# The first of twelve steps put in another order, and the sign of w_out's words set by VectorE

## The chip, the cores and the metric

The kernel runs on one core of one Trainium2 chip. The metric is the device time of one execution, in microseconds. Three unprofiled executions before the change took 602.38, 602.40 and 603.73 us; their median, 602.4 us, is the time before.

## What is computed

A recurrent attention layer (RWKV6) feeds a feed-forward block with an unusual gate:

```python
for t in range(S):                                   # S = 768, batch 4, 8 heads, head size 48
    kt, vt, rt, wt = k[:, :, t], v[:, :, t], r[:, :, t], w[:, :, t]
    cur = einsum('bhd,bhe->bhde', u * kt, vt)
    y[:, :, t] = einsum('bhd,bhde->bhe', rt, state + cur)
    state = wt[..., None] * state + einsum('bhd,bhe->bhde', kt, vt)
x = y.transpose(0, 2, 1, 3).reshape(3072, 384)
h = x @ w_in                                         # 384 -> 2048
g = h * erf(softplus(h))
out = g @ w_out                                      # 2048 -> 384
```

All inputs of the attention are fp32. `w_in` and `w_out` reach the kernel as doubles and are made fp32 on the chip.

## The kernel before

The work is cut into 12 steps; step s holds 128 tokens of two batch entries (16 heads). The recurrence is not run token by token. Inside a step the tokens are combined in levels 1 to 6 (spans of 2, 4, ... 64 tokens). For a level, TensorE makes 64 small products of r and k (`level_products`), VectorE then multiplies r and k by running products of w (`scale`), and VectorE or ScalarE takes the wanted part of the products into the tile `own` (`take_level`). The next level's products need the scaled r and k, and write into the other of two PSUM tiles, `pp0` and `pp1`, once its reader is done. The running products of w, the "totals", are made by GpSimd: one multiplication of neighbours per level, 512, 256, ... 16 columns wide, in `prepare`. After level 6 comes the end of the attention step: `from_own` (own times v), the transposes of K with the copies into `kT`, `state_part` (K times v, the new state), and `through_state` (the old state times r). The result goes into `xT`, and the feed-forward block of step s-1 (`hidden`, L947) and of step s-3 (`project`, L979, later `project_fast`, L1055) runs between the levels of step s. Steps 0 to 3 take all six levels this way; later steps do the near tokens on VectorE and GpSimd from other tiles (`rows`).

Every engine executes its own list in the order in which the program issues it: the kernel switches the scheduler off for all five engines, so the order in the source is the order on each engine, and an instruction that waits holds up all behind it on its engine. That goes for SyncE's list of loads too. Some loads are held back on purpose by a tiny GpSimd copy into the first word of the destination tile, which reads a tile that is written late (`load(i, behind)`, `load_v(s, behind)`, `wait_for`).

The weights come in 16 pairs of 128-row blocks, 0 to 7 of `w_in` and 8 to 15 of `w_out`, as pairs of 32-bit words. Each pair goes through stages that carry one letter: `l` loads the words (three buffers, `words`), `b` scales the high words on ScalarE into PSUM (L245), `r` scales the low words on ScalarE into `rest` (L254), `h` shifts the scaled high words left by three on VectorE (L262), `o` adds `rest` on GpSimd (L270), and `j` is `h` and `o`. Pairs 0 and 1 use the PSUM tiles `m` in two halves, the others the PSUM tile `y`, one after another. `b` is a Prelu whose slope for negative numbers puts the sign where the shift keeps it[...]. The table `CONVERT` says which stages run in steps 1, 2 and 3 at which level, each entry with two strings: ahead of `take_level`, and in `place`, behind it.

Step 0 (`attend_first`, L702) has no other work beside it but the first two weight pairs. `keep_busy` (L806) issues two matmuls of zeros, 384 and 192 columns wide, into a `pp` tile that nobody reads, one such pair in each of levels 2 to 5. The second half of step 0's state, `pending` (L789), is run in step 1.

Of the kernel before, what the change touches and what calls it, by code (L numbers as in the profile page):

```python
# [17 lines left out]
P = 128  # L18
# [43 lines left out]
def kernel(  # L62
# [105 lines left out]
    def load_second(behind):  # L168

        t = ins.tile([P, 2, JP, C], FP32, name="in")  # L170
        vt = ins.tile([P, NH, D], FP32, name="v")
        ws[1] = ins.tile([P, JP, C], FP32, name="w")
        loaded[1] = t, vt
        nc.scalar.copy(t[:, 0, 0, 0:1], behind)
        load_halves(t, rkw[1])
        nc.sync.dma_start(out=ws[1][:], in_=rkw[1][:, 2])

    def load_v(s, behind=None):

# [36 lines left out]
    def convert(weights):  # L216

        held = {}  # L220
        plain = weights[0][1].dtype == FP32

        def load(i, behind=None):
            if i >= len(weights):
                return
            dst, src = weights[i]
            if plain:
                nc.sync.dma_start(out=dst, in_=src)
                return
            words = wide.tile([P, 2, DM, 2], I32, name="words", bufs=3)  # L230
            if behind is not None:
                nc.gpsimd.tensor_copy(out=words[:, 0, 0, 0:1].bitcast(FP32), in_=behind)
            load_halves(words[:].rearrange("p i n two -> p i (n two)"), src.bitcast(I32))
            held[i] = {"words": words}

        def scale_high(i, part=slice(0, 2)):


            if i not in held:
                return  # L240
            if i < 2:
                base = ps_m.tile([P, NP * C], FP32, name="m")[:, :DM]
            else:
                base = y[:].rearrange("p e j q t -> p e (j q t)")[:, :, :DM]
            nc.scalar.activation(  # L245
                base, held[i]["words"][:, part, :, 1].bitcast(FP32), AF.Prelu,
                scale=2.0**-112, alpha=-(2.0**32),
            )
            held[i].setdefault("bases", []).append((base.bitcast(I32), part))

        def scale_low(i):
            if i in held:
                rest = wide.tile([P, 2, DM], I32, name="rest", bufs=2)
                nc.scalar.mul(  # L254
                    out=rest[:], in_=held[i]["words"][:, :, :, 0].bitcast(U32), mul=2.0**-29
                )
                held[i]["rest"] = rest

        def shift(i):
            if i in held:  # L260
                base, part = held[i]["bases"].pop(0)
                nc.vector.tensor_scalar(  # L262
                    out=weights[i][0].bitcast(I32)[:, part], in0=base, scalar1=3, scalar2=None,
                    op0=ALU.logical_shift_left,
                )

        def add(i):
            if i in held:
                into = weights[i][0].bitcast(I32)
                nc.gpsimd.tensor_tensor(  # L270
                    out=into, in0=into, in1=held.pop(i)["rest"][:], op=ALU.add
                )

        def join(i):
            shift(i)
            add(i)

        stages = {"l": load, "b": scale_high, "r": scale_low, "h": shift, "o": add, "j": join}
        done = {"l": 4, "b": 2, "r": 2, "j": 2}

        def send(what):
            for stage in what:
                stages[stage](done[stage])
                done[stage] += 1

        return stages, send
# [10 lines left out]
    def scale(s, level, batch=None, only=None):  # L297
# [23 lines left out]
            halves, halves, view(tots[level - 1], 0, [[1, n], [2, nb], [0, half]])  # L321
        )

    def prepare(s):


        in_t = loaded[s][0]
        if s < DIRECT:
            rk1 = att.tile([P, 2, JP, C], FP32, name="rk1", bufs=1)
            parts = 1 if s else NJ  # L330
            def multiply_u(i, x):
                n = slice(i * JP // parts, (i + 1) * JP // parts)
# [21 lines left out]
            if s < 2:  # L354
                for i in range(parts):
                    for x in range(2):
                        multiply_u(i, x)
                yield
            else:
                yield  # L360
                yield
                multiply_u(0, 0)

        tots, tot = [], ws[s][:].rearrange("p n t -> p (n t)")
        tot_sb = att.tile([P, JP * (C - NC)], FP32, name="tot_sb")
# [1 line left out]
        for level in range(1, LOG + 1):  # L367
# [4 lines left out]
            nc.gpsimd.tensor_mul(new, pair[:, :, 0], pair[:, :, 1])  # L372
            tot = new
            used += nb
            if level == (2 if s > 1 else 1) and s < DIRECT:
                yield
        if s < DIRECT:
            ready[s] = rk1, tots, tot
            yield
            if s >= 2:  # L380
                yield
                multiply_u(0, 1)
            return

        own = att.tile([P, NH, HC], FP32, name="own")
# [316 lines left out]
    def attend_first(xT):  # L702


        c, in_t, vt, made, S, S_next, ends = parts_of(0)
        K = in_t[:, 1]
        RK = in_t[:, 0:2]
        following = prepare(1)
        own = att.tile([P, NH, HC], FP32, name="own")
        halves = [range(j * NP, (j + 1) * NP) for j in range(NJ)]  # L710

        def wait_for(of):

            nc.gpsimd.tensor_copy(out=block_sb[:, 0:1], in_=of)

        pp = products([P, NE, JP, HC])
        for half in halves:
            level_products(pp, made[:], 1, half)
            stay_warm(2)
        nc.scalar.copy(first[:], mask_sb[:, 0, :])  # L720
        for j in range(NJ):
            scale(0, 1, batch=j)
        load_second(in_t[:, 0, JP - 1, 1:2])
        nc.vector.tensor_mul(
            own[:], pp[:].rearrange("p e n t -> p (e n) t"),
            first[:, None, :].to_broadcast([P, NH, HC]),
        )
        for level in range(2, LOG):
            pp = turns.pop("pp", None) or products([P, NE, JP, HC])
            level_products(pp, RK, level)  # L730
# [4 lines left out]
            if level == 2:  # L735
                stages["b"](0, 0)
                stages["b"](0, 1)
                stages["r"](0)
                next(following)
            elif level == 3:  # L740
                stages["l"](1, own[:, 0, 4:5])
                stages["h"](0)
            elif level == 4:
                load_v(0, own[:, 0, 8:9])
                stages["h"](0)
                stages["b"](1, 0)
                stages["b"](1, 1)
                stages["r"](1)
                wait_for(in_t[:, 0, JP - 1, 8:9])
                next(following)  # L750
        pp = turns.pop("pp")
        level_products(pp, RK, LOG)
        for only in (1, 0):
            scale(0, LOG, only=only)
        take_level(own, pp, LOG)
        stages["l"](2, own[:, 0, HC // 2 : HC // 2 + 1])
        stages["l"](3)

        kT = att.tile([P, NH, D], FP32, name="kT", bufs=1)
        kT_by_e = kT[:].rearrange("p (e n) d -> p e n d", e=NE)  # L760
        turned = []
        for half in halves:
            turned.append(products([P, NP, P]))
            for i, n in enumerate(half):
                nc.tensor.transpose(turned[-1][:, i, :], K[:, n, :], ident[:])
        from_own(0, own, 1)
        stages["h"](1)
        for half, ps, copy in zip(halves, turned, (nc.scalar.copy, nc.vector.tensor_copy)):
            copy(
                kT_by_e[:, :, half.start : half.stop],  # L770
                ps[:].rearrange("p n (e d) -> p e n d", e=NE)[..., :D],
            )
        fence()
        ps = [[products([P, NE, JP, HC], 1 - e)[:, e] for e in range(NE)]]
        state_part(0, kT, ps, (0,))
        from_own(0, own, 0)
        nc.scalar.copy(middle[rows(1)], ps[0][1][rows(1), :, :D])
        nc.vector.tensor_copy(middle[rows(0)], ps[0][0][rows(0), :, :D])
        stages["h"](1)
        wait_for(in_t[:, 0, JP - 1, HC - 1 : HC])  # L780
        stages["o"](0)
        nc.gpsimd.tensor_mul(faded[1][:], middle[:], ends[:, :, 1:2].to_broadcast([P, JP, D]))
        stages["o"](1)
        load_v(1, middle[:, 0, 0:1])
        for _ in following:
            pass
        through_state(0, xT)

        def pending():  # L789
# [13 lines left out]
                start=True, stop=True,  # L803
            )

    def keep_busy(pp):  # L806

        zeros = states[1][0][:].rearrange("p n d -> p (n d)")
        for n in (DM, DM // 2):
            nc.tensor.matmul(  # L810
                pp[:].rearrange("p e n t -> p (e n t)")[:, :n], lhsT=ident[:],
                rhs=zeros[:, :n], start=True, stop=True, skip_group_check=True,
# [2 lines left out]
    def attend(s, xT, early, place, behind):  # L815
# [11 lines left out]
        for level in range(near_log(s) + 1 if s == DIRECT else 1, LOG + 1):  # L827
# [9 lines left out]
            if level == LOG and s == DIRECT:  # L837
                spread_blocks(s + 1, pp)
            scale(s, level)
            early(level - 1)  # L840
            got = pp[:].rearrange("p e n t -> p (e n) t")
            if level == 1:
# [2 lines left out]
                )  # L845
            else:
                take_level(own, pp, level)
            if s == 1 and level == LOG - 2:
                turns.pop("pending")()
                load_v(2)  # L850
            if level > 1 and (s, level) != (DIRECT, LOG - 1):
                next(following, None)
            place(level - 1)
# [288 lines left out]
    def run_late(s, tokens, following=None):  # L1142
# [26 lines left out]

    CONVERT = (  # L1170
        (),
        (("j", "brl"),) * 5 + (("j", ""), ("", ""), ("", ""), ("", "brl")),
        (("j", "brl"),) * 5 + (("j", "l"), ("", ""), ("", ""), ("", "br")),
        (("j", "br"), ("j", "")),
    )

    STAGES = {
# [17 lines left out]
    with tc.manual_schedule(  # L1195
# [12 lines left out]
            ]  # L1208
        )
        stages["l"](0, loaded[0][0][:, 1, JP - 1, C - 1 : C])  # L1210
        for _ in prepare(0):
            pass
        for s in range(n_steps):
            xTs[s] = xs.tile([P, KT, UNIT], FP32, name="xT")
            places = iter(range(8))
# [149 lines left out]
```

## Time and profile before

| what | value |
|---|---|
| median of three executions | 602.4 us |
| the profiled execution | 606.16 us |
| its span, first to last instruction | 604.4 us |
| TensorE (matmul) busy | 587.1 us, 97% |
| VectorE busy | 431.3 us, 71% |
| ScalarE busy | 363.7 us, 60% |
| GpSimd busy | 272.2 us, 45% |
| granted TensorE clock, mean | 0.991 |
| step 0's first matmul of `hidden` (L947) starts | 34.12 us |

Durations and gaps come from the profiled execution, which is 3.8 us above the median. A row of the timeline has the start, the duration, the engine, the line, the operation, what is written and read, and, in brackets, how long the engine sat idle before it and what ended that. In tables by window the columns are the busy time of each engine with the number of its instructions, the granted TensorE clock (1.00 is full), and the share and rate of the DMA engines.

### The profile page before, as it was taken

The numbers are of one execution on the slowest core, as the hardware profiler recorded it, in microseconds if no ns is written. First come the engines' busy times: TensorE is split into PE (matmuls) and PEld (weight loads), VectorE is DVE, ScalarE is ACT, GpSimd is POOL, SyncE is SP. The second block draws the span as 40 slices with busy tenths as digits, with TensorE's granted clock in tenths as the row PEclk, the third lists the DMA queues.
The fourth block names the chain that finished last, engine by engine and source line by source line (L and its number), as shares of the span: only waits on it lengthen the run. The fifth ranks groups of instructions, "written<-read, shape, count | busy, mean of one in ns | idle before, by whom it ended". The sixth has DMA issues, their size and how long they took to land.

```text
span 604.4 us, 16605 instructions
## 1 busy us (share of the span) xinstructions
PE 587.1 (97%) x7262; PEld 503.2 (83%) x7262; DVE 431.3 (71%) x510; ACT 363.7 (60%) x475; POOL 272.2 (45%) x303
## 2 busy tenths in 40 slices
PE   8898989999999999999999999999999999999997
PEld 6676768668757867899899899899898898898997
DVE  6756377599998599899799799799799624124140
ACT  3546777735436288684864865864765764656710
POOL 4357138250549729929729629639539100000000
PEclk9889999999999999999999999999999999999999
DMA  6684193504034323524334334324331300000000
GB/s 232 202 301 149 42 347 121 214 17 144 17 134 159 71 104 110 128 101 169 72 104 168 72 104 168 71 104 133 72 106 53 72 8 27 2 21 13 2 26 28
DMA packets 53937, 63.24 MB, mean 105 GB/s; under 512 B 35144, under 2 KB 40424, under 8 KB 52840
## 3 DMA queue, kind: packets, MB, share of 16 engines
q1 hardware_dynamic: 53480, 61.98, 31.9%
q8 instruction: 57, 0.93, 0.6%
q10 hardware_dynamic: 384, 0.20, 0.1%
q14 instruction: 16, 0.13, 0.1%
HBM read 52.39 MB, written 8.69 MB: 101 GB/s over the span
## 4 chain that ended last, share of the span: by engine, by line
PE 73%; DVE 11%; ACT 3%; issue 2%; DMA 1%; SPq 1%; ACTq 0%; POOL 0%; DVEq 0%; POOLq 0%
PE m L947 33%; PE m L1055 28%; PE m L979 4%; DVE in L320 3%; PE pp L509 2%; PE y L543 2%; DMA words<-in_moe_w_out 1%; PE y L569 1%; DVE sums L424 1%; PE pp L615 1%; DVE h L936 1%; DVE words L438 1%; DVE rk L434 1%; DVE mixed L1003 1%; DVE own L521 1%
## 5 line engine op out<-in xcount | busy, mean ns | idle before, releaser
L947 PE MATMUL m<-xT,w_in_sb 128*128 128x256 f32 x1152 | 258.7, 383 | 3.7 <-ACT h L956 2.7
L947 PEld LDWEIGHTS m<-xT,w_in_sb 128*128 128x128 f32 x1152 | 217.2, 191 | 35.3 <-ACT h L956 2.9
L956 ACT COPY h<-m 128x512 f32<-128x512 f32 x96 | 55.8, 581 | 85.2 <-PE m L947 85.1
L320 DVE TENSOR_TENSOR in<-in,tot_sb 128x1024 f32<-128x1024 f32 (+1 forms) x59 | 82.5, 1399 | 21.1 <-PE pp L509 13.5
L434 POOL TENSOR_TENSOR rk<-words 128x528 f32<-128x528 f32 (+3 forms) x28 | 41.5, 1481 | 91.5 <-DVE sums L424 81.1
L438 POOL TENSOR_TENSOR words<-words,rest 128x528 f32<-128x528 f32 (+10 forms) x77 | 79.0, 1026 | 6.0
L979 PE MATMUL m<-w_out_sb,h 128*128 128x384 f32 x192 | 64.3, 491 | 1.0 <-DVE h L936 1.0
L979 PEld LDWEIGHTS m<-w_out_sb,h 128*128 128x128 f32 x192 | 35.7, 190 | 24.6 <-issue 1.1
L1055 PE MATMUL m<-mixed,h 128*128 128x192 f32 x288 | 51.1, 331 | 0.0
L1055 PE MATMUL m<-w_out_sb,h 128*128 128x192 f32 x288 | 50.3, 329 | 0.0
L903 ACT ACT_TABLE_LOAD x36 | 46.2, 1283 | 2.6 <-DMA xT<-y 2.0
L1055 PEld LDWEIGHTS m<-w_out_sb,h 128*128 128x128 f32 x288 | 46.9, 190 | 0.5
L1055 PEld LDWEIGHTS m<-mixed,h 128*128 128x128 f32 x288 | 46.6, 190 | 0.9
L907 ACT ACT_TABLE_LOAD x36 | 46.2, 1283 | 1.6 <-DVE room L1038 1.1
L509 PEld LDWEIGHTS pp<-in 48*64 48x64 f32 (+1 forms) x2368 | 33.7, 126 | 15.1 <-issue 7.3
L372 POOL TENSOR_TENSOR tot_sb<-tot_sb 128x256 f32<-128x256 f32 (+4 forms) x60 | 42.5, 708 | 4.5
L1055 PE MATMUL m<-w_out_sb,room 128*128 128x192 f32 x256 | 44.2, 326 | 0.0
L509 PE MATMUL pp<-in 48*64 48x64 f32 (+1 forms) x2368 | 38.2, 212 | 4.3 <-issue 1.5
L1055 PEld LDWEIGHTS m<-w_out_sb,room 128*128 128x128 f32 x256 | 42.0, 190 | 0.0
L912 DVE TENSOR_TENSOR h<-h,y 128x1024 f32<-128x1024 f32 x17 | 20.7, 1215 | 28.3 <-ACT y L907 28.2
L903 ACT ACTIVATE room<-h 128x1024 f32<-128x1024 f32 x36 | 38.1, 1057 | 0.4
L434 POOL TENSOR_TENSOR words<-words 128x336 f32<-128x336 f32 (+6 forms) x49 | 35.3, 719 | 3.8
(139 smaller groups left out, 800.7 us busy)
## 6 DMA issues: line engine op xcount, KB each, us to landing
in<-in_rkw SPq DMA_DIRECT2D x8, 1024.0 KB, 5.1
words<-in_moe_w_in SPq DMA_DIRECT2D x16, 384.0 KB, 5.4
words<-in_moe_w_out SPq DMA_DIRECT2D x16, 384.0 KB, 6.1
words<-in_rk_rows SPq DMA_DIRECT2D x8, 768.0 KB, 5.7
w<-in_rkw SPq DMA_DIRECT2D x11, 512.0 KB, 5.7
v<-in_v SPq DMA_DIRECT2D x12, 384.0 KB, 6.1
out<-o SPq DMA_DIRECT2D x24, 192.0 KB, 2.6
in<-in_rkw SPq DMA_DIRECT2D x7, 512.0 KB, 5.4
```

Of the source, the lines that this page charges most:

```text
L320: nc.vector.tensor_mul(halves, halves, view(tots[level - 1], 0, [[1, n], [2, nb], [0, half]]))
L372: nc.gpsimd.tensor_mul(new, pair[:, :, 0], pair[:, :, 1])
L434: engine.tensor_mul(terms[n], r[:, :, n:], k[:, :, : near - n])
L438: engine.tensor_mul(k[:, :, :m], k[:, :, :m], w[:, :, n : n + m])
L509: nc.tensor.matmul(pp[s0 : s0 + m, e, n, :m], lhsT=rk[rows(e), 1, n, s0 : s0 + m], rhs=rk[rows(e), 0, n, t0 : t0 + m], start=True, stop=True,)
L903: nc.scalar.activation(sp_room, chunks[0], AF.Softplus)
L907: nc.scalar.activation(at, sp_room, AF.Erf)
L912: nc.vector.tensor_mul(h, h, at)
L947: nc.tensor.matmul(ps[:, ff, :], lhsT=w_in_sb[:, g * FG + f + ff, kk * P : (kk + 1) * P], rhs=xT[:, kk, :], start=kk == 0, stop=kk == KT - 1,)
L956: nc.scalar.copy(h[:, f : f + FT, :], ps[:])
L979: nc.tensor.matmul(ps[j][:], lhsT=gs[g][:, f, j * C : (j + 1) * C], rhs=w_out_sb[:, g * FG + f, :], start=g + f == 0, stop=g == NG - 1 and ...
L1055: nc.tensor.matmul(to, lhsT=a[:, f], rhs=b[:, f], start=start and f == 0, stop=f == FG - 1, skip_group_check=True,)
```

## The change

- **GpSimd's totals of step 0** are no longer made in one go. `plan_totals` lays them out, and `attend_first` issues level 1 in two halves (one as soon as half of w is there, one behind the scaling of level 1), and levels 2 to 6 behind the scalings of levels 2, 3 and 4, each behind a `wait_for` copy. The totals of step 1 move behind the middle state.
- **Loads**: v of step 0 and w of step 1 are issued in level 2, behind the words of pair 1, whose load moves from level 3 to level 2. v of step 1 is issued ahead of pair 1's addition.
- **Pair 1's scalings** (`b`, `b`, `r`) move on ScalarE from level 4 to behind the copy of K; its first shift moves on VectorE behind the copies of K and of the state.
- **Transposes**: both halves of K's transposes now use the alternating `pp` tiles in the shape of the levels, and one unread 384-column matmul is put ahead of them.
- **`pending`** moves from level 4 to level 2 of step 1.
- **w_out's pairs** (8 to 15) are scaled by a plain multiplication, shifted in place in PSUM, and a second VectorE instruction (`scalar_tensor_tensor`) takes the sign bit out of the high word and joins it. The `words` buffer of such a pair is so read until then. In steps 2 and 3 these pairs' `j` moves from ahead of `take_level` to behind it. Pair 9's words are loaded in step 1, one place earlier, and with it all later pairs.

```diff
@@ convert @@
-            nc.scalar.activation(
-                base, held[i]["words"][:, part, :, 1].bitcast(FP32), AF.Prelu,
-                scale=2.0**-112, alpha=-(2.0**32),
-            )
+            high = held[i]["words"][:, part, :, 1].bitcast(FP32)
+            if i < signed:
+                nc.scalar.activation(base, high, AF.Prelu, scale=2.0**-112, alpha=-(2.0**32))
+            else:
+                nc.scalar.mul(out=base, in_=high, mul=2.0**-112)
...
+                into = weights[i][0].bitcast(I32)[:, part]
                 nc.vector.tensor_scalar(
-                    out=weights[i][0].bitcast(I32)[:, part], in0=base, scalar1=3, scalar2=None,
+                    out=into if i < signed else base, in0=base, scalar1=3, scalar2=None,
                     op0=ALU.logical_shift_left,
                 )
+                if i >= signed:
+                    nc.vector.scalar_tensor_tensor(
+                        out=into, in0=held[i]["words"][:, part, :, 1], scalar=-(1 << 31),
+                        in1=base, op0=ALU.bitwise_and, op1=ALU.bitwise_or,
+                    )
@@ plan_totals (new) @@
+        for level in range(1, LOG + 1):
+            tots.append(tot)
+            nb = JP * C >> level
+            new = tot_sb[:, used : used + nb]
+            pairs.append((new, tot.rearrange("p (n two) -> p n two", two=2)))
...
+        def go_on(*levels, part=slice(None)):
+            for level in levels:
+                new, pair = pairs[level - 1]
+                nc.gpsimd.tensor_mul(new[:, part], pair[:, part, 0], pair[:, part, 1])
@@ attend_first @@
+        totals(1, part=slice(0, batch))
         for j in range(NJ):
             scale(0, 1, batch=j)
         load_second(in_t[:, 0, JP - 1, 1:2])
...
+        wait_for(1)
+        totals(1, part=slice(batch, 2 * batch))
...
+        behind = {2: (2,), 3: (3, 4), 4: (5, 6)}
...
-                next(following)
-            elif level == 3:
-                stages["l"](1, own[:, 0, 4:5])
+                for _ in prepare(1):
+                    pass
+                stages["l"](1, own[:, 0, 2:3])
+                nc.sync.dma_start(out=vt[:], in_=v[0])
+                nc.sync.dma_start(out=ws[1][:], in_=rkw[1][:, 2])
+            elif level < LOG - 1:
                 stages["h"](0)
-            elif level == 4:
-                load_v(0, own[:, 0, 8:9])
-                stages["h"](0)
-                stages["b"](1, 0)
-                stages["b"](1, 1)
-                stages["r"](1)
...
+            if level in behind:
+                wait_for(1 << level - 1)
+                totals(*behind[level])
...
-        for half in halves:
-            turned.append(products([P, NP, P]))
+        turned = [products([P, NE, JP, HC])]
+        keep_busy(turned[0], (DM,))
+        for j, half in enumerate(halves):
+            if j:
+                turned.append(products([P, NE, JP, HC]))
...
+        stages["b"](1, 0)
+        stages["b"](1, 1)
...
+        stages["r"](1)
         stages["h"](1)
+        stages["h"](1)
...
+        load_v(1, middle[:, 0, 0:1])
+        totals(1)
         stages["o"](1)
-        load_v(1, middle[:, 0, 0:1])
+        totals(*range(2, LOG + 1))
@@ attend @@
+            if s == 1 and level == 2:
+                turns.pop("pending")()
+                load_v(2)
             early(level - 1)
...
-            if s == 1 and level == LOG - 2:
-                turns.pop("pending")()
-                load_v(2)
@@ CONVERT, from step 1 on @@
-        (("j", "brl"),) * 5 + (("j", ""), ("", ""), ("", ""), ("", "brl")),
-        (("j", "brl"),) * 5 + (("j", "l"), ("", ""), ("", ""), ("", "br")),
-        (("j", "br"), ("j", "")),
+        (("j", "brl"),) * 5 + (("j", "l"), ("", ""), ("", ""), ("", "brl")),
+        (("", "jbrl"),) * 5 + (("", "j"), ("", ""), ("", ""), ("", "br")),
+        (("", "jbr"), ("", "j")),
```

## The prediction

> **What bounds the kernel now.** I read the page first (who is busy in which slice), then the chain of waits, then the timeline of the first 180 us for each wait of TensorE, last the granted clock by window.
>
> ```profile
> PE   8898989999999999999999999999999999999997
> DVE  6756377599998599899799799799799624124140
> PEclk9889999999999999999999999999999999999999
> ```
>
> A slice is 15.1 us. TensorE shows 9 from the seventh slice on; only in the first 123 us does it wait for more than 0.3 us, and only there does its clock dip. Behind that the chain of waits runs on VectorE from 119 to 180 us (its shared work of steps 3 and 4), with one TensorE gap of 0.30 us at 179.84, and on TensorE to the end. So microseconds saved before step 3 move the end one for one. All edits lie in steps 0 to 3.
>
> The timeline of step 0's end:
>
> ```profile
> 22.57 1.29 DVE L314 TENSOR_TENSOR in<-in,tot_sb 128x512 f32<-128x512 f32 x2 [0.28 <-PE pp L509]
> 22.79 0.52 ACT L245 ACTIVATE m<-words 128x384 f32<-128x384 f32 x1 [1.88 <-DMA words<-in_moe_w_in]
> 23.24 0.90 ACT L254 ACTIVATE rest<-words 128x768 int32<-128x768 uint32 x1
> 23.32 0.66 PE L765 MATMUL pp<-ident,in 128*128 128x128 f32 x4 [0.84 <-DVE in L314]
> 24.04 1.15 ACT L528 COPY own<-pp 32x512 f32<-32x512 f32 x2
> 25.24 0.66 PE L765 MATMUL pp<-ident,in 128*128 128x128 f32 x4 [1.27 <-ACT own L528]
> 30.28 2.93 PE L583 MATMUL y<-y,mixed 128*128 128x256 f32 x6
> 34.12 2.86 PE L947 MATMUL m<-xT,w_in_sb 128*128 128x256 f32 x12
> ```
>
> Level 6's products end at 22.48, but L528 starts at 24.04: ScalarE is in pair 1's scalings, which waited for their words. The second transposes need L528. And six matmuls at L583 take 2.93 us where twelve of the same size take 2.86 at L947: half clock, as the windows say:
>
> ```profile
> 24.00:27.00 3.00, 1.61 (x52) 1.33 (x54) 1.07 (x3) 1.66 (x4) 1.75 (x3) 1.00 0.19 28
> 27.00:30.00 3.00, 3.00 (x118) 3.00 (x115) 2.15 (x3) 0.85 (x2) 1.85 (x2) 0.53 0.96 356
> 30.00:33.00 3.00, 3.00 (x21) 2.00 (x14) 0.00 (x0) 0.00 (x0) 3.00 (x4) 0.50 0.38 146
> 57.00:60.00 3.00, 3.00 (x19) 2.45 (x10) 2.09 (x2) 1.15 (x2) 1.91 (x3) 0.65 0.02 5
> ```
>
> The clock is halved from 27.15 to 33.98 (6.83 us) and from 57.87 to 61.28 (3.41 us), each time behind about 3.4 us in which TensorE idled 1.3 to 1.5 us. Step 1's waits:
>
> ```profile
> 50.81 1.16 PE L509 MATMUL pp<-in 48*64 48x64 f32 x64 [0.87 <-DVE s L793]
> 56.42 0.68 PE L509 MATMUL pp<-in 48*32 48x32 f32 x55 [1.46 <-issue]
> 57.03 4.54 PE L947 MATMUL m<-xT,w_in_sb 128*128 128x256 f32 x12
> ```
>
> And step 2's:
>
> ```profile
> 72.27 1.28 ACT L245 ACT_TABLE_LOAD   x1 [1.72 <-issue]
> 82.48 2.86 PE L947 MATMUL m<-xT,w_in_sb 128*128 128x256 f32 x12 [1.77 <-ACT h L956]
> 85.10 0.87 ACT L245 ACTIVATE y<-words 128x768 f32<-128x768 f32 x1 [2.67 <-DMA words<-in_moe_w_out]
> 87.33 2.86 PE L947 MATMUL m<-xT,w_in_sb 128*128 128x256 f32 x12 [0.90 <-ACT h L956]
> 87.47 2.89 DVE L320 TENSOR_TENSOR in<-in,tot_sb 128x1024 f32<-128x1024 f32 x1
> ```
>
> **Step 0, totals.** L307's second half took 1.50 us beside GpSimd's 512-wide total, the first 0.69: a half-width total costs it about 0.4 less. But level 3's scaling, 0.09 us behind `take_level` 2 before, now waits for three GpSimd instructions that themselves wait for that take: starts of tiny copies 0.12 apart (two), a 256-wide total (0.6, the shortest row), hand-overs about 0.15; 1.0 us, so 0.9 later. Net +0.5. Levels 4 to 6 find their totals done: `wait_for` follows the scaling, and about 0.7 us of GpSimd fits into the 1.3 us until the next. The later totals of step 1 free L320 at 20.28 of 0.16. Products 6: +0.35, ending at 22.8.
>
> **Step 0, transposes.** L528 starts at once, 22.95 to 24.1. K's scaling ends at 23.55; the unread matmul is two thirds of a pair that takes 1.21, so 0.8 us, and ends at 23.6: hidden, 0.05 at most. The second transposes start at 24.15 instead of 25.24, `from_own` at 24.75 (25.83), `state_part` at 25.6 (26.61), since its copies of K no longer wait. Pair 1's two scalings (0.53 each) fit on ScalarE in front of the copy of the state at 26.5; its `r` (0.9) ends at 27.9, as the next copy, L576, becomes due. L569 starts at 27.1 instead of 28.38: **-1.3**. v, issued 3 us earlier, is there.
>
> **Step 0, clock.** From L569 to L947 passed 5.74 us. At full clock L569 is 0.66, L576 0.37, L583 half of 2.86, L589 0.92, hand-overs 0.3: 3.7. That is -2.0 more. [...] The row shows the clock halved behind just these gaps[...]; with only some 0.5 us idle left I take the row. Against that, TensorE reaches its next instructions sooner, and the instruction queue's packets (one at 29.82) lie behind the weights' loads: I subtract 0.7. Step 0: **-2.6** (ends -3.3 and -1.1).
>
> **Step 1.** `pending` at level 2 puts its adds directly behind the scaling; level 3's products come only after 2.8 us of L947, so 0.87 goes. The 1.46 of "issue": an instruction packet of TensorE's queue starts at 53.99, just as the DMA load falls from 1.0 to 0.2. Loads of step 2 start about 4 us earlier (v of step 1 no longer waits for pair 1's addition), so this backlog is gone by then and the packet early. Without the stall the clock stays up: 4.54 - 2.79 = 1.75. Together **-4.1** (ends -4.1 and 0).
>
> **Step 2, gains.** One table load less on ScalarE, and words one pair ahead, take away most of 1.77 and 0.90 (with two small waits, 3.3 us in all). [...] the row is 1.28, and the scaling starts at its end, 73.57. Two switches save 2.6 by the row[...], and only where ScalarE holds up L956.
>
> **Step 2, costs.** Six pairs gain a second VectorE instruction. No such instruction is in the trace; the nearest is L262, same size, one PSUM input: 0.95 us, 0.87 from start to start. Its ends: 0.87, and twice that, since L521, also with short strides, takes 1.34 instead of 0.71. I take 0.87. VectorE's round per level becomes 1.14 + 0.62 + 0.87 + 0.87 = 3.5 us against TensorE's 3.88 (L947 2.79 with L509 1.09). It fits until GpSimd's addition collides: L320 at 87.47 took 2.89 instead of 1.23 because L270 had started at 87.45. The addition now starts where the scaling does. I count one such collision in three, 0.55 per level, 0.2 over TensorE's round, and as much for `take_level` 2 and for ScalarE, whose next scaling waits for the joined word with L956 and L528 queued behind it: about 2.0 us over the six levels. Net **-1.3** (ends -3.3 and +3.3).
>
> **Step 3.** Two more, 1.75 us on the chain's VectorE stretch; one table load less lets the first pair fall into VectorE's idle 4.8 us before 113.78, the wait of 0.77 before 118.57 goes. **-0.3** (ends -1.0 and +2.5).
>
> **Sum.** -2.6 - 4.1 - 1.3 - 0.3 = -8.3 on the profiled execution: 606.16 to 597.9, its span 604.4 to 596.1. The median is 3.8 lower than that execution; the stall at 56.42 with its clock is 3.2 and may well be missing there, so I count it half: -8.3 + 1.6 = -6.7, and 602.4 becomes **595.7**.
>
> **Rivals.**
> - *VectorE takes it back* (0.17): collisions eat step 2's gain and step 1's stall was never in the median: -2.6 - 0.9 = -3.5, 598.9. For it: VectorE at 9 tenths; against: its round has 0.38 us of room.
> - *The unread matmul does not hold the clock, and the stall moves instead of going* (0.08): step 0 -1.1, step 1 -0.9, step 2 and 3 zero: 600.4 to 601.5, no change.
> - *All waits go* (0.15): step 0 -3.3, steps 1 to 3 -4.1 - 2.5 - 0.5: 592.
> - *Slower: GpSimd's addition wins every level* (0.10). Then the round is 3.5 + 1.66 = 5.2, 1.3 over TensorE's for five levels, 6.6 less the 3.3 of waits removed; step 3 adds 2.5. With step 0 and 1 at their weak ends, -2.0, it is +3.8: 606.2. It decides once a round is over 4.9 us.
>
> **How the numbers follow.** The forecast has 0.50, with a range of its own of 593.5 to 598. About 0.3%, 1.8 us, can be told from no change. Faster: 0.50 + 0.17 + 0.15 = 0.82; same 0.08; slower 0.10. The range, 591 to 601.5, leaves out the slower case and the edge of the best one.
>
> **What would show it.** Right: L528 at about 22.9, no half clock between 24 and 34, L947's first start near 31.5; no "issue" gap in step 1; L956 not waited for in step 2; the second instruction at 0.95 us. Wrong: level 3's scaling over 1 us late, clock 0.5 behind step 0, L320 over 2 us at most levels of step 2, or TensorE waiting for VectorE in steps 2 and 3.

## The result, and the profile after

The changed kernel takes 599.58 us (median of six executions, 598.23 to 600.20), the kernel before beside it 602.52 (601.02 to 603.73): ratio 0.9947, 95% interval 0.9928 to 0.9966. That is 2.9 us faster. 595.7 was forecast, 6.7 us faster: the direction was right, the gain less than half. The profiled execution takes 599.54 us with a span of 597.7.

The page's slices, as shown of before:

```profile
PE   8889999999999999999999999999999999999997
DVE  6757498799996799799799799799799525023140
PEclk9989999999999999999999999999999999999999
```

The clock still dips, one slice later (30 to 45 us), and TensorE is still short of 9 in the first three slices. The timeline of step 0 (start, duration, engine, line, operation, operands, and the idle time before it):

```profile
14.71 1.23 DVE L327 TENSOR_TENSOR in<-in,tot_sb 128x1024 f32<-128x1024 f32 x1 [0.96 <-POOL tot_sb L349]
...
21.92 1.16 ACT L556 COPY own<-pp 32x512 f32<-32x512 f32 x2 [2.82 <-PE pp L537]
22.73 1.09 PE L798 MATMUL pp<-ident,in 128*128 128x128 f32 x8
27.40 1.56 PE L611 MATMUL y<-y,mixed 128*128 128x256 f32 x6
30.34 0.68 PE L537 MATMUL pp<-rk 48*64 48x64 f32 x26 [1.11 <-issue]
30.94 2.86 PE L985 MATMUL m<-xT,w_in_sb 128*128 128x256 f32 x12
```

Lines have moved: L985 is L947 of before, L611 is L583, L556 is L528, L327 is L320, L643 is L615, L994 is L956. The copy of level 6 starts at 21.92 without waiting for ScalarE, the transposes run as one block, L611 takes 1.56 us at full clock instead of 2.93, and step 1's first expert matmul starts at 30.94 instead of 34.12. Level 3's scaling waits 0.96 us for its total, as the prediction had it (1.0). Then step 1:

```profile
34.72 0.74 PE L643 MATMUL pp<-v,kT 64*48 64x48 f32 x25
37.90 0.38 PE L643 MATMUL pp<-v,kT 64*48 64x48 f32 x7 [2.44 <-issue]
38.21 4.29 PE L985 MATMUL m<-xT,w_in_sb 128*128 128x256 f32 x12
```

In the middle of the pending work TensorE stops for 2.44 us with nothing that the profile shows as a reason, and the twelve matmuls behind it take 4.29 us instead of 2.86. The windows (busy time of TensorE's matmuls and weight loads, VectorE, ScalarE, GpSimd; granted clock; DMA share; GB/s):

```profile
30.00:33.00 3.00, 2.66 (x36) 2.36 (x37) 2.09 (x2) 2.83 (x4) 2.69 (x7) 1.00 0.89 316
33.00:36.00 3.00, 2.46 (x93) 1.98 (x91) 0.98 (x1) 1.17 (x2) 1.75 (x1) 1.00 0.95 334
36.00:39.00 3.00, 1.10 (x11) 0.96 (x12) 0.91 (x3) 0.00 (x0) 0.00 (x0) 1.00 0.68 260
39.00:42.00 3.00, 3.00 (x10) 2.29 (x8) 2.75 (x3) 1.54 (x2) 1.43 (x1) 0.58 0.91 299
```

The DMA engines are 0.89 to 0.95 busy from 30 to 36 us; the clock is halved from 39.47 to 42.89. The trace shows what came in before TensorE went on. Queue 8, listed as "instruction", moved 57 packets of 16 KB in this execution, and as many in that of before; one of them starts at 35.43 and takes 0.89 us, and TensorE goes on 1.58 us after its end. Call each weight load, matmul and semaphore instruction of TensorE a record, and count them in order of time: TensorE stops in front of record 1474 here, and in front of record 1986, at 56.42, in before. The difference, 512, would be two packets of 256 records, and the total fits: 57 packets for 14,634 records. From these counts I estimate which packet brings which record: packet k those from 194 + 256k on. The profiles of before and after agree with it: in all 112 cases record 194 + 256k starts 1.30 us or more after the end of packet k. Records 1218, 1474, 1730 and 1986 are those of packets 4 to 7, and the packet that starts at 35.43 is the fifth.

Step 2 came out better than forecast:

```profile
81.11 0.95 DVE L269 SCALAR_TENSOR_TENSOR w_out_sb<-words,y 128x768 int32<-128x768 int32 x1
81.67 2.86 PE L985 MATMUL m<-xT,w_in_sb 128*128 128x256 f32 x12
81.98 1.22 DVE L327 TENSOR_TENSOR in<-in,tot_sb 128x1024 f32<-128x1024 f32 x1
82.21 2.68 POOL L277 TENSOR_TENSOR w_out_sb<-w_out_sb,rest 128x768 int32<-128x768 int32 x1 [0.94 <-DVE w_out_sb L269]
```

The new second instruction takes 0.95 us, as assumed, and ScalarE's table load ahead of the first scaling of this step (1.28 us at 72.27 in before) is gone. GpSimd's addition now starts just behind the scaling, which keeps its 1.22 us; the addition takes 2.68 instead of 1.83, and nothing in step 2 waits for it.

### The profile page after: what moved, and what is told of

The parts are those of the page before. It is cut to its first block, busy times and chain, and to the rows that moved or that the text cites. A ratio compares the mean times of both kernels' runs of the same rounds, so it can differ in the third digit from the quotient of the medians.

```text
span 597.7 us, 16615 instructions
## 1 busy us (share of the span) xinstructions
PE 583.5 (98%) x7264; PEld 500.3 (84%) x7264; DVE 436.6 (73%) x518; ACT 361.6 (60%) x473; POOL 270.9 (45%) x306
## 4 chain that ended last, share of the span: by engine, by line
PE 80%; DVE 13%; DMA 3%; issue 2%; ACT 1%; POOL 0%; SPq 0%; DVEq 0%; POOLq 0%; ACTq 0%
PE m L985 36%; PE m L1093 28%; PE m L1017 5%; PE pp L537 4%; DVE in L327 3%; PE y L571 2%; PE pp L643 2%; PE y L597 1%; DVE h L974 1%; DVE own L549 1%; DVE words L466 1%; DVE sums L452 1%; DVE y L264 1%; DVE rk L462 1%; DMA rest<-in_w_rows 1%
## 5 line engine op out<-in xcount | busy, mean ns | idle before, releaser
L985 PE MATMUL m<-xT,w_in_sb 128*128 128x256 f32 x1152 | 258.7, 383 | 1.0 <-DMA xT<-y 0.9
L985 PEld LDWEIGHTS m<-xT,w_in_sb 128*128 128x128 f32 x1152 | 216.9, 191 | 32.7 <-issue 1.3
L994 ACT COPY h<-m 128x512 f32<-128x512 f32 x96 | 55.7, 581 | 83.2 <-PE m L985 83.2
L327 DVE TENSOR_TENSOR in<-in,tot_sb 128x1024 f32<-128x1024 f32 (+1 forms) x59 | 78.3, 1327 | 26.1 <-PE pp L537 16.1
L950 DVE TENSOR_TENSOR h<-h,pp 128x1024 f32<-128x1024 f32 x19 | 23.0, 1213 | 19.5 <-ACT pp L945 19.5
```

The source lines that it names most:

```text
L327: nc.vector.tensor_mul(halves, halves, view(tots[level - 1], 0, [[1, n], [2, nb], [0, half]]))
L950: nc.vector.tensor_mul(h, h, at)
L985: nc.tensor.matmul(ps[:, ff, :], lhsT=w_in_sb[:, g * FG + f + ff, kk * P : (kk + 1) * P], rhs=xT[:, kk, :], start=kk == 0, stop=kk == KT - 1,)
L994: nc.scalar.copy(h[:, f : f + FT, :], ps[:])
```

## Where the profiled executions gained

Each column is the time between two starts on TensorE: step 0 to the first expert matmul of step 1, step 1 to that of step 2, step 2 to the first product with w_out in step 3, step 3 to the products of step 4 behind their wait. What is left, 424.4 to 425.1 us in every profile, hardly differs. The ratios are those of the timed executions to the kernel before beside them; the clock is the mean over a kernel's executions (for before, over all that stand beside the experiments).

| kernel | step 0 | step 1 | step 2 | step 3 | ratio (95%) | clock |
|---|---|---|---|---|---|---|
| before | 34.12 | 38.48 | 36.19 | 71.05 | | 0.9944 |
| `b_again` (before) | 30.84 | 39.32 | 37.60 | 71.23 | 0.9999 (0.9983, 1.0015) | 0.9948 |
| after | 30.94 | 38.50 | 33.62 | 70.14 | 0.9947 (0.9928, 0.9966) | 0.9977 |
| `after_again` | 31.62 | 37.95 | 33.63 | 70.88 | 0.9933 (0.9911, 0.9955) | 0.9977 |
| `hold2` | 31.54 | 36.78 | 33.62 | 70.07 | 0.9918 (0.9894, 0.9942) | 0.9992 |
| `v_late` | 31.48 | 35.54 | 33.64 | 71.03 | 0.9916 (0.9896, 0.9937) | 1.0000 |
| `pend4` | 31.60 | 34.89 | 33.24 | 71.24 | 0.9898 (0.9873, 0.9923) | 0.9993 |
| `pend3` | 31.08 | 34.86 | 34.17 | 70.74 | 0.9876 (0.9856, 0.9896) | 0.9996 |
| `pend3_again` | 31.43 | 34.66 | 33.63 | 71.05 | 0.9887 (0.9869, 0.9905) | 0.9995 |
| `pend3_prelu` | 31.86 | 35.57 | 36.12 | 70.50 | 0.9944 (0.9923, 0.9965) | 0.9978 |
| `pend2_only` | 32.09 | 35.62 | 35.34 | 70.52 | 0.9950 (0.9934, 0.9965) | 0.9961 |
| `step0_only` | 31.10 | 35.44 | 36.52 | 71.16 | 0.9953 (0.9935, 0.9971) | 0.9974 |
| `wout_only` | 31.95 | 40.44 | 34.00 | 70.89 | 0.9980 (0.9961, 0.9999) | 0.9921 |
| `prelu` | 31.29 | 39.65 | 37.07 | 71.42 | 0.9982 (0.9957, 1.0007) | 0.9963 |
| `all_but_step0` | 31.16 | 34.07 | 33.66 | 70.44 | 0.9897 (0.9863, 0.9932) | 0.9983 |

## The experiments

The expectations call their theories by letters or numbers; each says what it holds.

**How steady is the kernel before?** `b_again` is before without an edit.

> The kernel before, unchanged, once more. Theory A (the forecast's step from profile to median was too small: the profiled execution of before was an unusually slow one): the new execution has a span of 599 to 602 us, with a mean clock of 0.995 or more, so at most one half-clock stretch, and it lacks either the halving behind step 0 (27 to 34 us) or the 1.46 us of issue in step 1. Theory B (every execution has them, and the 3.6 us lie outside the span): the span is again 604 +- 0.5 and the clock 0.991, with half clock at 27 to 34 and at 58 to 61 us.

604.54 us; in its profile:

```profile
54.05 0.68 PE L509 MATMUL pp<-in 48*32 48x32 f32 x55 [1.46 <-issue]
54.66 4.54 PE L947 MATMUL m<-xT,w_in_sb 128*128 128x256 f32 x12
```

The stall in front of record 1986 is the same 1.46 us with the same 4.54 behind it: no accident of one execution. But step 0 ends at 30.84 without any half clock (L583 takes 1.56 us), as early as in the changed kernel. The 129 executions of before that stand beside the experiments run from 601.0 to 608.3 us, median 604.1, mean clock 0.9944; only 18 of them have a clock of 0.9985 or more. The first medians, 602.4 and 602.5, lie low in that spread.

**The changed kernel beside the same executions.**

> The changed kernel unaltered, beside the kernel before on the same chip. Theory A (it gains 4 to 5 us, and the six first runs of the kernel before were low for it): ratio 0.991 to 0.993, about 599.5 where the kernel before is at 604. Theory B (it gains 2.9 us and no more): ratio 0.995, about 601.3. On either, records 1218 and 1474 of TensorE are the ones in front of which it waits for nothing shown; A expects the half clock in step 1 in fewer than all executions.

600.23 us against 604.21, 4.0 us faster; the two intervals overlap. The stall at record 1474 is there again, 1.89 us.

**The loads behind the stall.** `hold2` lets the loads of r, k and w of step 2 wait for level 2's scaling of step 1:

```diff
+                load_step(2, in_t[:, 0, JP - 1, 2:3])
...
-            if s + 2 < n_steps:
+            if s and s + 2 < n_steps:
```

> After, with the loads of step 2 (r and k, w, two small ones) held behind level 2's scaling of step 1 instead of following v of step 1 at once. Theory 1 (TensorE runs out of instructions at 37.9 us because its instruction packets wait behind one burst of loads from 28 to 36 us): the 2.44 us of issue inside pending goes or falls under 0.5, an instruction packet starts before 33 us, the clock is not halved at 39.5, and the time falls by 2.5 to 4 us to 595.5 to 597. Theory 2 (the stall belongs to pending's new place, whatever is loaded): the gap of 2.4 us stays at the same products and the time stays at 599.6.

598.92 us. TensorE's rows (L645, L988 and L997 are here L643, L985 and L994 of after):

```profile
36.58 0.38 PE L645 MATMUL pp<-v,kT 64*48 64x48 f32 x7 [0.52 <-issue]
...
50.41 2.83 PE L988 MATMUL m<-xT,w_in_sb 128*128 128x256 f32 x12 [1.33 <-ACT h L997]
```

The stall shrinks to 0.52 and the clock holds (1.0 in the mean of this profile), but 1.33 us come back at 50.41, where ScalarE was late because it had waited 6.76 us for weight words. So the time lies above the expected 595.5 to 597. `v_late` moves one line only, v of step 1, and with it all that stands behind it in SyncE's list (v is issued at 31.62 instead of 28.20, the first load of step 2 at 32.06 instead of 28.64):

```diff
-        load_v(1, middle[:, 0, 0:1])
         totals(1)
         stages["o"](1)
+        load_v(1, middle[:, 0, 0:1])
```

> The changed kernel with one line moved: v of step 1 is asked for behind pair 1's addition again, some 3 us later, and the loads of step 2 behind it. If the early loads hold up the instruction packet: the DMA share falls under 0.6 between 30 and 33 us, the packet starts near 33 us instead of 35.4, no gap over 1 us in front of record 1474, no half clock there, ratio 0.988 to 0.991. If the place of the pending work alone decides: the gap of about 2 us stays, ratio 0.993 or more.

Its windows, TensorE's rows from the same stretch on, and the row of ScalarE that made it late:

```profile
30.00:33.00 3.00, 2.12 (x33) 1.90 (x34) 1.45 (x2) 2.85 (x6) 2.84 (x5) 1.00 0.16 37
33.00:36.00 3.00, 3.00 (x103) 2.56 (x101) 1.08 (x2) 1.85 (x3) 2.24 (x4) 1.00 0.96 297
```

```profile
35.26 0.89 PE L643 MATMUL pp<-v,kT 64*48 64x48 f32 x32
36.08 2.86 PE L985 MATMUL m<-xT,w_in_sb 128*128 128x256 f32 x12
...
42.94 0.88 ACT L247 ACTIVATE y<-words 128x768 f32<-128x768 f32 x1 [7.98 <-DMA words<-in_moe_w_in]
...
45.24 1.96 PE L985 MATMUL m<-xT,w_in_sb 128*128 128x256 f32 x8 [1.33 <-ACT h L994]
```

With the load gone from 0.89 to 0.16 in the window from 30 to 33, the packet starts at 32.21 instead of 35.43 and the pending work runs through record 1474 in one piece. So here the early loads held the packet up, by 3.2 us. The time, 598.13 us at 0.9916, lies just above the expected range, though: at 45.24 TensorE waits 1.33 us for ScalarE, whose scaling ahead of L994 waited for words that now come later. The loads held up the packet in the changed kernel, and the words in this one.

**The place of the pending work.** `pend4` puts it back at level 4, `pend3` and `pend3_again` at level 3:

```diff
-            if s == 1 and level == 2:
+            if s == 1 and level == 3:
                 turns.pop("pending")()
                 load_v(2)
```

> After, with pending put back to level 4 of step 1. Theory 1 (instructions wait behind the loads): the gap of about 2.4 us stays at the same count of TensorE's instructions, so it now falls into level 3's products or the matmuls of L985 around them, and the 0.87 us of waiting for pending's additions comes back in level 5: 600 to 601 us. Theory 2 (pending's place): the gap of 2.4 us and the half clock behind it go, the 0.87 comes back: 596.5 to 597.5.

> The changed kernel with the pending state's second half at level 3 of step 1 instead of level 2. Theory A (TensorE's record 1474 must not be reached within about 2.4 us of the instruction packet's start; 32 short matmuls at level 2 bring it there 2 us too soon, one level of expert matmuls in front of them does not): no gap over 1 us between 34 and 42 us and no half clock there, ratio 0.989 to 0.991 as with the work at level 4. Theory F (each level earlier costs, through the adds on VectorE): halfway, 0.9915.

> The version with the pending work at level 3 once more, as the base of the next two: ratio 0.986 to 0.990, clock full in nearly all executions.

597.37, 596.70 and 597.18 us: faster than the kernel before and the changed one, at level 3 with intervals wholly below both of the changed kernel's. Step 1 in `pend3`, by timeline and by window:

```profile
34.96 2.86 PE L985 MATMUL m<-xT,w_in_sb 128*128 128x256 f32 x12
37.75 1.16 PE L537 MATMUL pp<-in 48*64 48x64 f32 x64
38.84 0.92 PE L643 MATMUL pp<-v,kT 64*48 64x48 f32 x32
```

```profile
36.00:39.00 3.00, 3.00 (x80) 2.48 (x80) 2.69 (x3) 0.00 (x0) 1.44 (x1) 1.00 1.04 406
```

The loads are as dense as in the changed kernel and the packet starts only 0.8 us earlier, at 34.62. But ahead of the pending work now stand twelve expert matmuls: 24 records in 2.8 us, where the pending work's 25 short ones use up 50 in 0.74. TensorE gets to record 1474 at 37.93 instead of 35.46, some 2.5 us later, and its packet is there.

`pend2_only` is the move to level 2 in the kernel before, and nothing else.

> The kernel before with the pending work at level 2 and nothing else. Theory A (64 records of short matmuls ahead of record 1474 while the loads of step 2 lie in the queues): a gap of about 2 us without a releaser in front of record 1474 between 34 and 42 us, a ratio of 1.000 or more. The prediction's account (-4.1 from the move and the earlier loads together; the loads are not earlier here): 0.9985 from the 0.87 us alone.

This went against the expectation that the stall comes with the place: 600.65 us, 0.9950. Its window shows why, and so do TensorE's rows:

```profile
30.00:33.00 3.00, 2.51 (x40) 1.87 (x39) 0.32 (x1) 2.15 (x5) 2.92 (x5) 1.00 0.11 34
```

```profile
35.86 0.89 PE L615 MATMUL pp<-v,kT 64*48 64x48 f32 x32
36.68 2.86 PE L947 MATMUL m<-xT,w_in_sb 128*128 128x256 f32 x12
```

Without step 0's edits the loads of step 2 leave a hole at 30 to 33 us (share 0.11), the packet slips in at 32.84, and there is no stall. The move to level 2 alone gains 3 us; it takes the early loads and the early place together to lose them.

**w_out's pairs.** `prelu` gives the changed kernel the old scaling, the old places of `j` and pair 9's load in its old place; `wout_only` gives before the new ones; `pend3_prelu` undoes the edit with the pending work at level 3, where the stall at 1474 was gone (0.67 us of it are back in this profile).

```diff
-        signed = len(weights) // 2
+        signed = len(weights)
...
-        (("", "jbrl"),) * 5 + (("", "j"), ("", ""), ("", ""), ("", "br")),
+        (("j", "brl"),) * 5 + (("j", "l"), ("", ""), ("", ""), ("", "br")),
```

> After, with w_out's pairs as before: Prelu, one VectorE instruction, their stages ahead of take_level in steps 2 and 3, and pair 9's words loaded one place later. What w_out's edit is worth in the profile is 2.5 us in step 2 and 1.0 in step 3. Theory 1 (that gain is its own): step 2 takes 36 us again from its first feed-forward matmuls behind xT to the first of L1017, the two waits for h come back, 602 to 603 us. Theory 2 (VectorE's and ScalarE's earlier state, brought by steps 0 and 1, made it): step 2 stays at 33.7 us and the time at 599.6 to 600.2.

> The kernel before with the edit of w_out's pairs alone (the scaling without Prelu, the second VectorE instruction, the joining one step later). Theory A (this edit is worth what returning it cost, about 3.5 us): 600 to 601, ratio 0.993 to 0.995, the first product of step 3 comes 2 to 3 us earlier relative to the first expert matmul of step 2. Theory C (it pays only because the other edits start step 2 with less behind it): under 1.5 us, ratio over 0.9975.

> The same with w_out's pairs as before (Prelu, the joining in the same step). If the edit is worth the 3.3 us by which step0_only and the version with the pending work at level 4 differ: ratio 0.992 to 0.994, the first product with w_out in step 3 comes 2 to 3 us later behind the first expert matmul of step 2. If it is worth its 1.2 us alone: 0.989 to 0.990.

602.48, 602.81 and 600.70 us. The edit is worth 1.2 us alone (1 - 0.998 of 604) and 3.4 in company (0.9944 - 0.9887). In the traces it is 2.0 to 3.6 us of step 2 each time, against the profiles of the same kernel without or with it. `pend3_prelu` shows what goes:

```profile
77.24 2.86 PE L985 MATMUL m<-xT,w_in_sb 128*128 128x256 f32 x12 [1.59 <-ACT h L994]
82.41 2.86 PE L985 MATMUL m<-xT,w_in_sb 128*128 128x256 f32 x12 [1.22 <-ACT h L994]
82.58 2.55 DVE L327 TENSOR_TENSOR in<-in,tot_sb 128x1024 f32<-128x1024 f32 x1
```

These two waits for ScalarE, and the collision of L327 with the addition, are gone with the edit. Alone it keeps step 1's stall in front of record 1986 (1.50 us in `wout_only`), and its executions have the lowest clock of all, 0.9921: 0.0023 below before, which over 603 us is an estimated 1.4 us given back. In its profile the half clock follows step 0's gaps (from 22.80), a wait of 1.43 us for VectorE at 45.09, and the stall; whether the edit brings these about was not tried.

**Step 0's edits, together and one by one.** `step0_only` is the changed kernel with `prelu`'s and `pend4`'s edits, so that only step 0's edits are left. Three more take single ones out: `no_unread` drops `keep_busy(turned[0], (DM,))`, `pair_early` puts pair 1's `b`, `b`, `r` back into level 4, `totals_first` makes all totals of step 0 at the start.

> The changed kernel with w_out's pairs as before and the pending work back at level 4: what is left are the totals tied to the scalings, weight pair 2's place, the unread matmul and the loads. Theory A (the edits add up; step 0 gives its 3.2 us in each execution in which the clock was halved there, less where it was not): 601.5 to 602.5 where the kernel before is at 604, ratio 0.9955 to 0.998. Theory D (what step 0 gains TensorE gives back to the instruction queue behind it): ratio 0.999 or more.

> The changed kernel without the unread matmul ahead of the transposes. If the matmul holds the clock: half clock for 3.4 us or more between 24 and 34 us, some 2 us longer, ratio 0.996 or more where the changed kernel has 0.993. If the shorter gaps alone hold it: full clock there, the same time as the changed kernel within 0.5 us.

> The changed kernel with weight pair 1's scalings and its rest back in level 4 of step 0, ahead of the last level's copies on ScalarE. If their place is what brings the transposes forward: the copy of the last level's products starts up to 1 us later again, TensorE waits over 1 us for it and step 0 ends about 1.3 us later, with half clock behind it in some executions; ratio 0.995 to 0.997 where the changed kernel has 0.993. If pair 1's words are there in time now (they are asked for a level earlier): no difference over 0.3 us.

> The changed kernel with all totals of step 0 back at the start, not tied to the scalings. By the prediction's sum (the tie costs 0.5 net): the first expert matmul of step 1 comes 0.5 us earlier, ratio lower by 0.001. If the tie is a gain: later by 0.5 us or more, for VectorE's first scalings take up to 1.50 us beside a 512-wide total again.

Together they gain 2.8 us (0.9953). One by one none is worth anything that can be measured: 0.9932 (0.9903, 0.9961), 0.9931 (0.9903, 0.9958) and 0.9926 (0.9900, 0.9951), against the changed kernel's 0.9933. With `pair_early` the copy of level 6 still starts at once, at 22.45: pair 1's words, asked for a level earlier, are scaled by then. For the unread matmul two more kernels drop it from `pend4` and `pend3`:

> The pending work at level 4 and no unread matmul ahead of the transposes. If the unread matmul is worth nothing also where no stall follows: ratio within 0.001 of 0.9898, clock full between 24 and 34 us. If it holds the clock: half clock there in some executions and 0.992 or more.

> The same without the unread matmul ahead of the transposes. If that matmul holds the clock: a mean clock lower by 0.002 or more over the executions, half clock in some of them, ratio 0.991 to 0.994. If the work's place alone decides: ratio within 0.0015 of pend3_again.

The first gave 0.9941 (0.9921, 0.9961), which spoke for the matmul; the second 0.9886 (0.9864, 0.9908) against 0.9887, at a mean clock of 0.9997. In `pend3_bare`:

```profile
23.59 1.09 PE L797 MATMUL pp<-ident,in 128*128 128x128 f32 x8 [0.84 <-DVE in L321]
```

```profile
21.00:24.00 3.00, 1.92 (x72) 1.38 (x70) 2.72 (x4) 1.15 (x2) 0.00 (x0) 1.00 0.20 76
24.00:27.00 3.00, 2.65 (x103) 2.21 (x101) 1.52 (x5) 1.93 (x5) 2.14 (x3) 1.00 0.56 154
```

The gap of 0.84 is open again and the clock stays at 1.00. In `pend4_bare` the clock was full there too; its profile stalled elsewhere, 1.42 us in front of record 1730 at 46.13, behind which the clock fell (0.997 in the mean of this profile). Why its twenty executions spread from 596.1 to 604.4 stays open. Last, `all_but_step0`: before with the pending work at level 3 and w_out's edit.

> The kernel before with the pending work at level 3 and the edit of w_out's pairs: all of the best version but step 0's edits. If these are worth the 2.8 us of step0_only: ratio 0.993 to 0.994, with half clock in step 0 in most executions. If they bring nothing beside the other two: 0.989 as pend3_again.

596.81 us, 0.9897 (0.9863, 0.9932): inside the interval of `pend3_again`, at the edge of that of `pend3`. Beside the other two, step 0's edits bring nothing that can be told.

## Why the prediction was half right

**Step 0, -2.6.** The profile seems to confirm it: L985 3.2 us earlier, L611 at full clock, level 3's scaling late by the amount foreseen. The experiments don't; that agreement was luck, for the profile of before was one with half clock in step 0. With the old step 0, half clock falls into it in three of five profiles (from 27.15, 22.80 and 24.86), with the new one in none of fifteen, three of them without the unread matmul. So the clock's term was of the right kind, but no execution has to lose 2.0 us: the old step 0 ends at 34.12, 30.84, 31.95, 32.09 and 31.16, mean 32.0, the new one at 31.45 in the mean, 0.6 earlier. The gain of `step0_only`, 2.8 us, is of the size forecast and sits for the most part elsewhere: its step 1 takes 35.44 us against 38.48 and 39.32, since the stall in front of record 1986 is missing. The row on which the prediction rested, 0.84 and 1.27 us of idle time ahead of the half clock, was not enough to credit the unread matmul: it fills the 0.84, which ended at 23.32, before the 3.4 us ahead of 27.15 that the prediction itself counts; and in `pend3_bare` the clock stays at 1.00 behind a gap of 0.84 alone. In step 1 the clock was halved behind single stalls of 1.46 us (before) and 2.44 us (after).

**Step 1, -4.1: the step that failed.** "Loads of step 2 start about 4 us earlier (v of step 1 no longer waits for pair 1's addition), so this backlog is gone by then and the packet early." The stall did go from 56.42, but the early loads put the backlog over the packet two further up the list, and the pending work at level 2 used up the last 50 records ahead of that place within 0.74 us; TensorE stopped there for 2.44 us and then ran at half clock for 3.41 us. Step 1 took 38.50 us against 38.48: 0, not -4.1. The terms of the sum were right in size: with the work at level 3 step 1 takes 34.86 and 34.66, 3.6 and 3.8 less, and the kernel is 6.5 to 7.5 us faster, about what was forecast. The rival that the stall moves instead of going had its chance at 0.08, and only together with losses elsewhere; in step 1 it is what happened.

**Step 2, -1.3.** Measured -2.6 (33.62 against 36.19). The gains and the 0.95 us were right; the cost of 2.0 for collisions with the addition was too large: L327 takes 1.22 to 1.42 us at all five levels, so with its head start (0.2 us in the rows shown) the scaling kept its time and the addition took longer (2.68 instead of 1.83). The slower rival, in which the addition wins each level, falls with that. (Its sum has slips: -2.0 is not the sum of the weak ends of steps 0 and 1, -1.1 and 0, and the 4.9 us leave out step 3's 2.5.)

**Step 3, -0.3.** 70.14 against 71.05 in the first profiles, but all kernels lie between 70.07 and 71.42, in no order that follows the edits: not to be told.

**From the profile to the median.** I counted the stall at 56.42 and its clock only half, as the median was 3.8 us below the profile. The stall stands in all three profiles in which the kernel's first two steps are the old ones (`before`, `b_again`, `wout_only`), with half clock behind it, and the 129 executions have their median at 604.1: so it belongs to the kernel, and the first medians were low. This error made the forecast smaller and so hid part of the other.

**The sum.** The gains of the parts don't add: alone, the move of the pending work gains 3.0 us, step 0's edits 2.8 and w_out's 1.2, 7.0 in all; together 2.9 to 4.0. The first two each take away the same stall in front of record 1986, and together they make the one at 1474. By the parts above, -0.6 for step 0 in the mean, 0 for step 1 and -2.6 for step 2 make -3.2, which lies between the 2.9 and 4.0 us measured.

## What to carry to other kernels

A gap that the profile puts down to nothing can lie at the boundary of an instruction packet. The evidence for it here: the records at which TensorE stopped lie a multiple of 256 apart (1218, 1474 and 1986), and it went on 1.43 to 1.58 us behind the end of a packet. Where that is found, count the records to the next such place, and don't put a run of short matmuls ahead of it while loads fill the queues: 50 records in 0.74 us, at a DMA share of 0.95, ended in the stall of 2.44 us. An earlier load is no gain by itself: ask which packet and which words it now delays. Before two edits' gains are added, ask whether they remove the same wait, and take the clock's dips from several executions, not one.

## What the runs showed of the hardware

In before TensorE stopped in front of record 1986 for 1.46 us, in after in front of 1218 for 1.11 and of 1474 for 2.44 us; it went on 1.50, 1.43 and 1.58 us after the transfer of that record's packet (0.93, 0.92 and 0.89 us) had ended. Stalls at the same products, with no releaser either, stand in the timelines of other kernels: those of 1218 with 0.93 us in `b_again`, 1.49 in `after_again`, 0.96 in `v_late`, 1.05 in `pend4`, 0.52 in `pend3`, 0.97 in `totals_first` and 0.49 in `pend2_only`; those of 1474 with 1.89 in `after_again` and `pair_early`, 2.44 in `prelu` and 0.52 in `hold2`; those of 1986 with 1.46 in `b_again` and 1.50 in `wout_only`. Which of them it was differed with the loads (`v_late`) and with how fast the records ahead of it went by (`pend3`). The clock fell to half for 3.41 us behind single gaps of 1.46 (before) and 2.44 us (after), and for 6.83 us behind the 0.84 and 1.27 of the old step 0 (before); in `wout_only` it fell at 22.80 behind 0.75 and 0.85; but not always: in before TensorE idled 1.77 us ahead of 82.48 and 0.90 ahead of 87.33, and the clock stayed at 1.00. Where the limit lies was not measured.
